# Attention by pairs of blocks in four 64x64 quadrants, the first two token tiles interleaved by quarters of the hidden units, and a new planned order

## The chip, the core and the metric

The kernel runs on one core of a Trainium2 chip. The engines are TensorE (PE in the profile, its weight loads PEld), VectorE (DVE), ScalarE (ACT), GpSimd (POOL) and SyncE (SP), which issues the DMAs. The metric is the device time of one launch in microseconds: 595.18 us, the median of three runs (594.43 to 595.61).

## The reference, cut to what matters

Two computations follow each other. A linear attention with per-channel decay runs over 4 batches, 8 heads, 768 tokens and 48 channels; its output, 3072 tokens by 384 channels, goes through a feed-forward layer of 2048 hidden units with a rational activation. All of it is float32.

```python
for t in range(S):
    cur = np.einsum('bhd,bhe->bhde', u[None] * kt, vt)
    y[:, :, t] = np.einsum('bhd,bhde->bhe', rt, state + cur)
    state = w[None, :, :, None] * state + np.einsum('bhd,bhe->bhde', kt, vt)
...
h = x @ w_in                      # 384 -> 2048
P = a[0] + a[1] * h + a[2] * h2 + a[3] * h3
Q = 1.0 + np.abs(b[0]) * np.abs(h) + np.abs(b[1]) * h2
return ((P / (Q + 1e-06)) @ w_out).astype(np.float32)
```

## The kernel before

**Attention.** A block is 128 tokens of one batch; there are 24, numbered so that blocks n and n+1 with n even are the same stretch of two batches, and block n+4 continues block n. For a block, k and r are scaled by powers of the decay (`scale_k`, `scale_r`), transposed on TensorE (`trans`: four 128x128 transposes into tk or tr) and copied out of PSUM (`trk_ev`, `trr_ev`). `a_pe` multiplies k by r within sub-blocks of 64 tokens: 16 small products per block, heads in pairs, one head of a pair in rows 0 to 63 of the array and the other in rows 64 to 127, each into the opposite half of the output partitions. `a_ev` masks the result (L452). `kv_pe` (L472, L473) forms k times v for the first 64 tokens and then again for all 128; `kv_ev` adds the old state (L487); `y_pe` (L500) multiplies by state and masked scores together; `y_ev` (L505) adds the bonus term, which `bonus_a`, `bonus_b`, `bonus_sum` and `bonus_v` make (L396, L401, L406, L410). `carry` (L511) decays the state for the next block of the batch. Small float32 matmuls show as two records each in the trace.

**Weights.** The weights come in as 64-bit floats. 28 pieces (12 of w_in, 16 of w_out) are loaded, turned into float32 by integer steps on ScalarE, VectorE and GpSimd, and split into a high and a low part (`cv_...`; L282 and L306 are two of the steps). `pieces` has them in four groups of seven, one group for each quarter of the hidden units.

**Feed-forward layer.** Two blocks make a token tile of 256 tokens, 12 tiles. A tile is worked through in 8 units `SL[s]` of 256 hidden units (JG = 2 groups of 128), 96 units in all, of which the last is split in two. Per unit: `f1` (18 matmuls of 128x256 per half of it, nine each, L541), five steps on ScalarE (z, q, t, ln, ex), five on VectorE (u3 L596, hi L602, p L606, d L612, lo L616) and `f2` (12 matmuls of 128x384, L545 to L547), which adds into two PSUM banks o0 and o1 over the 8 units of a tile; then `put_out` (L650, L652) copies them out and `put_dma` stores them. x is transposed and split for each tile by `xt_pe`, `xt_hi`, `xt_lo`.

**Order.** All of this is a list of tasks with a priority number, an estimated cost, dependencies and buffers. `run()` plays it through as a list scheduler: whenever an engine is free, the task of smallest number that fits is taken. The result is a fixed order on each engine, which the engine then follows in order; at run time each instruction waits on semaphores. Tasks that two engines could do go to the one that takes them first. While nothing else is ready, small bf16 matmuls into o1 ("warm", L1009) are put on TensorE until the first f2. The tables `AT` (blocks), `CT` (pieces), `OFF` (kinds of task) and `X0`, `DX0` to `DX2` (units) hold the numbers. `GFREE` and `GTIME` decide whether the step lo goes to GpSimd; with `GTIME` at 754.72 all 97 go to VectorE.

```python
p_ = pat("a", n)
o = slice(p * P + e * HALF, p * P + (e + 1) * HALF)
nc.tensor.matmul(p_[HALF:P, o], kt[0:HALF, p, c], ya[0:HALF, p, c], start=True, stop=True)
nc.tensor.matmul(p_[0:HALF, o], kt[HALF:P, p, c], yb[HALF:P, p, c], start=True, stop=True)
```

Of the kernel before, what the change touches and what calls it, by code (L numbers as in the profile page):

```python
# [30 lines left out]


@with_exitstack
def tile_linear_attention_rational_ffn(ctx, tc, r, k, v, w, u, w_in, w_out, a, b, out):
# [286 lines left out]
    rh, kh, ysa, ysb, vs = ([], [], [], [], [])  # L321
    vs2 = [cst.tile([P, 5, 2, NP, D], F32, name=f"vs{i}") for i in range(B // 2)]
    for i in range(3):
        for lst, nm in ((rh, "rh"), (kh, "kh")):
            lst.append(cst.tile([P, NP, 2, HALF], F32, name=f"{nm}{i}"))
    kt = cst.tile([P, NP, P], F32, name="kt")
    for i in range(2):
        for lst, nm in ((ysa, "ysa"), (ysb, "ysb")):
            lst.append(cst.tile([P, NP, P], F32, name=f"{nm}{i}"))
# [24 lines left out]
    def att_load(n, what):  # L354
# [5 lines left out]
        else:  # L360
            t, src = (hv(kh[n % 3]), k) if what == "k" else (hv(rh[n % 3]), r)
# [32 lines left out]
    def bonus_a(n, e):
        m = at.tile([P, H, D], F32, tag="m", name=f"m{n}", bufs=NM)
        e.tensor_mul(m, hv(rh[n % 3]), hv(kh[n % 3]))  # L396
# [15 lines left out]
    def trans(n, src, nm):  # L412
        p_ = pat(nm, n)
        for p in range(NP):
            nc.tensor.transpose(p_[:, ts(p, P)], src[:, p].rearrange("t a d -> t (a d)"), ident)  # L415
# [5 lines left out]
    def trk_ev(n, e):  # L421
        copy(e, kt.rearrange("p a t -> p (a t)"), state[n]["tk"])

    def trr_pe(n):
        trans(n, rh[n % 3], "tr")

    def trr_ev(n, e, half):
        y_, rows = ((ysa, slice(0, HALF)), (ysb, slice(HALF, P)))[half]
        copy(e, y_[n % 2][rows].rearrange("p a t -> p (a t)"), state[n]["tr"][rows])

    def a_pe(n):
        p_ = pat("a", n)
        ya, yb = ysa[n % 2], ysb[n % 2]
        for p in range(NP):
            for e in range(2):
                c = slice(e * HALF, (e + 1) * HALF)
                o = slice(p * P + e * HALF, p * P + (e + 1) * HALF)
                nc.tensor.matmul(p_[HALF:P, o], kt[0:HALF, p, c], ya[0:HALF, p, c], start=True, stop=True)  # L438
                nc.tensor.matmul(p_[0:HALF, o], kt[HALF:P, p, c], yb[HALF:P, p, c], start=True, stop=True)
        state[n]["a"] = p_  # L440

    def a_rows(n, half):
        return ((ysa[n % 2], slice(HALF, P)), (ysb[n % 2], slice(0, HALF)))[half]


    def a_ev(n, half, e):
        y_, rows = a_rows(n, half)
        av = state[n]["a"][rows]
        if e is nc.scalar:
            copy(e, y_[rows].rearrange("p a t -> p (a t)"), av)  # L450
            return
        nc.vector.tensor_mul(  # L452
            y_[rows].rearrange("p a (e t) -> p (a e) t", e=2), av.rearrange("p (c t) -> p c t", t=HALF),
            mask[rows].unsqueeze(1).to_broadcast([HALF, 2 * NP, HALF]),
        )

    def a_mask(n, half):
        y_, rows = a_rows(n, half)
        yv = y_[rows].rearrange("p a t -> p (a t)")
        nc.gpsimd.affine_select(  # L460
            yv, yv, pattern=[[0, 2 * NP], [1, HALF]], base=-1, channel_multiplier=-1,
            compare_op=ALU.is_ge, fill=0.0,
        )

    def kv_pe(n):
        d = state[n]
        p_ = pat("kv", n)
        k_, v_ = kh[n % 3], d["v"]
# [665 lines left out]
```

## Time and profile before

| | |
|---|---|
| median of the runs | 595.18 us |
| span of the profiled execution, first to last instruction | 593.4 us |
| TensorE busy, share of the span | 563.1 us, 95% |
| VectorE busy | 517.7 us, 87% |
| ScalarE busy | 435.5 us, 73% |
| GpSimd busy | 166.5 us, 28% |

The profiled execution's span is 1.8 us below the median of the runs. "Busy" is the time in which at least one instruction of the engine ran; matmuls are pipelined, so that a matmul's own duration is longer than the distance to the next one's start, and it is that distance that a row of matmuls costs. The mean durations of a group are of single instructions.

### The profile page before, as it was taken

Reading aid. Unit: us, or ns where it says so; the run is one execution under the profiler, and the core shown is the slowest. Engines: PE = TensorE matmul, PEld = TensorE weight load, DVE = VectorE, ACT = ScalarE, POOL = GpSimd, SP = SyncE. Lnnn points to the kernel's source line nnn. Section 1 sums busy time; section 2 is a strip of 40 time slices with the busy share of each in tenths; the row PEclk is TensorE's granted clock in tenths of the full one; section 3 lists DMA queues with packets and bytes.
Section 4 is the critical chain, followed back from the end, with each engine's and each line's share of the span. In section 5 each row is a group of like instructions: output and inputs, shape, how many; then the busy total and the mean of one; then the engine's idle time right before and its main releaser. Section 6 shows DMA issues by size and latency. Waiting matters only on the chain.

```text
span 593.4 us, 14638 instructions
## 1 busy us (share of the span) xinstructions
PE 563.1 (95%) x5991; PEld 540.8 (91%) x5991; DVE 517.7 (87%) x825; ACT 435.5 (73%) x729; POOL 166.5 (28%) x189
## 2 busy tenths in 40 slices
PE   8899696789999999999999999999999999999995
PEld 8799585778999999999999999999999999999995
DVE  5999998999999997889899888898888998888882
ACT  7679876978862785777677878865778785888780
POOL 6698976664135121013040010143001010000000
PEclk9999888989999999999999999999999999999999
DMA  7687653551222230012020003021003000000000
GB/s 189 163 224 193 166 142 92 127 109 32 55 53 57 68 75 8 2 41 54 28 55 2 27 1 73 10 42 43 14 0 81 2 15 15 0 28 2 28 1 31
DMA packets 95807, 34.85 MB, mean 59 GB/s; under 512 B 89074, under 2 KB 92148, under 8 KB 95732
## 3 DMA queue, kind: packets, MB, share of 16 engines
q1 hardware_dynamic: 95732, 33.83, 23.4%
q8 instruction: 49, 0.80, 0.6%
q14 instruction: 26, 0.21, 0.1%
HBM read 29.11 MB, written 4.72 MB: 57 GB/s over the span
## 4 chain that ended last, share of the span: by engine, by line
PE 71%; DVE 3%; ACT 1%; issue 1%
PE h L541 29%; PE o L545 11%; PE o L546 10%; PE o L547 10%; PE y L500 2%; PE a L438 2%; PE kv L472 2%; PE x L519 1%; PE tk L415 1%; PE tr L415 1%; DVE h L596 1%; DVE q L606 0%; DVE g L602 0%; DVE vs L511 0%; ACT t L583 0%
## 5 line engine op out<-in xcount | busy, mean ns | idle before, releaser
L541 PE MATMUL h<-xth,wi_hi 128*128 128x256 f32 x576 | 166.2, 289 | 0.0
L541 PE MATMUL h<-xtl,wi_hi 128*128 128x256 f32 x576 | 161.6, 281 | 0.0
L541 PE MATMUL h<-xth,wi_lo 128*128 128x256 f32 x576 | 161.5, 280 | 0.0
L545 PE MATMUL o<-wo_hi,g 128*128 128x384 f32 x384 | 134.8, 351 | 0.0
L547 PE MATMUL o<-wo_hi,g 128*128 128x384 f32 x384 | 130.4, 339 | 1.4 <-DVE g L616 1.4
L546 PE MATMUL o<-wo_lo,g 128*128 128x384 f32 x384 | 130.1, 339 | 0.0
L572 ACT ACTIVATE q<-h 128x512 f32<-128x512 f32 (+1 forms) x97 | 57.4, 591 | 83.3 <-PE h L541 63.0
L541 PEld LDWEIGHTS h<-xth,wi_hi 128*128 128x128 f32 x576 | 109.0, 189 | 1.2
L541 PEld LDWEIGHTS h<-xtl,wi_hi 128*128 128x128 f32 x576 | 109.2, 190 | 0.0
L541 PEld LDWEIGHTS h<-xth,wi_lo 128*128 128x128 f32 x576 | 108.8, 189 | 0.0
L602 DVE SCALAR_TENSOR_TENSOR g<-h,sig,z 128x512 fp32r<-128x512 f32 (+1 forms) x97 | 72.0, 743 | 28.1 <-ACT z L592 25.8
L578 ACT ACTIVATE w<-q,off,root 128x512 f32<-128x512 f32 (+1 forms) x97 | 75.8, 781 | 2.9 <-DVE q L606 2.7
L596 DVE SCALAR_TENSOR_TENSOR h<-t,sig,h 128x512 f32<-128x512 f32 (+1 forms) x97 | 72.0, 742 | 3.2 <-ACT t L583 2.9
L583 ACT ACTIVATE t<-h,off,root 128x512 f32<-128x512 f32 (+1 forms) x97 | 74.7, 770 | 0.1
L547 PEld LDWEIGHTS o<-wo_hi,g 128*128 128x128 f32 x384 | 72.6, 189 | 2.4 <-DVE g L616 2.4
L612 DVE SCALAR_TENSOR_TENSOR h<-h,sig,q 128x512 f32<-128x512 f32 (+1 forms) x97 | 72.7, 750 | 2.3
L606 DVE SCALAR_TENSOR_TENSOR q<-w,sig,g 128x512 f32<-128x512 f32 (+1 forms) x97 | 72.1, 743 | 2.6
L545 PEld LDWEIGHTS o<-wo_hi,g 128*128 128x128 f32 x384 | 72.6, 189 | 1.4
L546 PEld LDWEIGHTS o<-wo_lo,g 128*128 128x128 f32 x384 | 72.7, 189 | 0.0
L592 ACT ACTIVATE z<-z,lnb 128x512 f32<-128x512 f32 (+1 forms) x97 | 69.9, 721 | 2.3
L588 ACT ACTIVATE z<-w,lnb 128x512 f32<-128x512 f32 (+1 forms) x97 | 66.4, 685 | 3.6 <-POOL wi_lo L306 1.1
L616 DVE TENSOR_TENSOR g<-h,z 128x512 fp32r<-128x512 f32 (+1 forms) x97 | 65.7, 679 | 0.7
(147 smaller groups left out, 932.0 us busy)
## 6 DMA issues: line engine op xcount, KB each, us to landing
sto<-in_moe_w_out_dram SPq DMA_DIRECT2D x16, 384.0 KB, 3.7
sti<-in_moe_w_in_dram SPq DMA_DIRECT2D x12, 512.0 KB, 5.2
rh<-in_r_dram SPq DMA_DIRECT2D x24, 192.0 KB, 3.7
kh<-in_k_dram SPq DMA_DIRECT2D x24, 192.0 KB, 3.3
vn<-in_v_dram SPq DMA_DIRECT2D x24, 192.0 KB, 3.4
out_dram<-os SPq DMA_DIRECT2D x24, 192.0 KB, 1.9
vs<-in_v_dram SPq DMA_DIRECT2D x24, 96.0 KB, 3.5
wraw<-in_w_dram SPq DMA_DIRECT2D x1, 1.5 KB, 2.3
```

The costliest lines, as they stand in the source:

```text
L541: nc.tensor.matmul(o, wt_[:, cc, ts(j, P)], x_[:, cc], start=(n == 0), stop=(n == 3 * NCC - 1))
L545: nc.tensor.matmul(o, hi, wo_hi[:, j], start=(j == 0), stop=False)
L546: nc.tensor.matmul(o, hi, wo_lo[:, j], start=False, stop=False)
L547: nc.tensor.matmul(o, lo, wo_hi[:, j], start=False, stop=(j == NJ - 1))
L578: nc.scalar.activation(g["w"], w_, AF.Square, scale=RB, bias=KB)
L583: nc.scalar.activation(g["t"], g["h"], AF.Square, scale=RA, bias=KA)
L588: nc.scalar.activation(g["z"], g["w"], AF.Ln, scale=2.0 ** -LN_SHIFT, bias=lnb[:, 2:3])
L592: nc.scalar.activation(g["z"], g["z"], AF.Exp, scale=-1.0, bias=lnb[:, 1:2])
L596: nc.vector.scalar_tensor_tensor(g["h"], g["t"], KAP, g["h"], op0=ALU.add, op1=ALU.mult)
L602: nc.vector.scalar_tensor_tensor(g["hi"], g["h"], c0, g["z"], op0=ALU.add, op1=ALU.mult)
L606: nc.vector.scalar_tensor_tensor(g["q"], g.get("w", g["q"]), qe, g["hi"].bitcast(F32), op0=ALU.add, op1=ALU.mult)
L612: nc.vector.scalar_tensor_tensor(g["d"], g["h"], c0, g["q"], op0=ALU.add, op1=ALU.subtract)
```

## The change

**Pairs and quadrants.** Attention tasks are per pair of blocks (m = 0 to 11) where they were per block. `a_pe(m)` issues 32 products: for both blocks, four head pairs, two sub-blocks e and two heads q, with head q's rows 0 to 47 or 64 to 111 of the array and the output in the half of the partitions that e gives, in one PSUM bank per head. So four successive products lie in four different 64x64 quadrants; before, two successive ones lay in two. `kv_pe(m)` issues 32 products of the same kind (two sub-blocks by two heads); the sum over 128 tokens is not formed by the array any more but by a second `kv_ev` step. The last pair of each batch pair (m = 10, 11) needs only the first sub-block, 16 products. `a_ev` is four steps per pair of 64x512, `kv_ev` four of 48x384, `carry` two of 48x384; before it was two per block in each case, `carry` with 48x192. Transposes give 112 rows, not 128. `y_pe`, the bonus steps, scaling and loads stay per block. r has two buffers, not three.

**Interleaving.** Units 0 to 15, two tiles' worth, go quarter by quarter: two units of tile 0, two of tile 1, two of tile 0 and so on. f2 opens and closes its accumulation at each change of tile: `put_out` then copies a partial output to SBUF (tag m) or adds to it there, 16 steps for these two tiles where it was 4. f1 waits only for the pieces of w_in, f2 for those of w_out.

**Order.** `order_of` replaces `run()`: the same kind of list scheduler with numbers of its own in `PRM`, a bonus `MB` for staying in a tile mode, and `SIDE`, which names the units (20 to 96) whose step lo goes to GpSimd. For these `ew_d` writes to SBUF.

```diff
+ 'DG': 7.55,
...
+ 'NT': 2,
...
+ 'X': (158.93, 16.6, 7.22, 6.95)}
...
+            bonus = prm["MB"] if e == "P" and mode else 0.0
+            ranked = sorted((key[i] - (bonus if tasks[names[i]]["mode"] == mode else 0.0), i) for i in ready[e])
+            i = next((i for _, i in ranked if allowed(i, e, now)), None)
...
-    def a_pe(n):
...
+    def a_pe(m):
+        ps = [pat("a", (m, q)) for q in range(2)]
+        for x in range(2):
+            for p in range(NP):
+                for e in range(2):
+                    c = ts(e, HALF)
+                    for q in range(2):
+                        nc.tensor.matmul(
+                            ps[q][c, ts(x * NP + p, HALF)], kt[RROWS[q], x, p, c], ys[q][RROWS[q], x, p, c], start=True, stop=True
+                        )
...
+    def kv_pe(m):
+        last = m // 2 == NB - 1
+        ps = [pat("kv", (m, e)) for e in range(1 if last else 2)]
...
+                for e, p_ in enumerate(ps):
+                    for q in range(2):
+                        nc.tensor.matmul(
+                            p_[RROWS[q], ts(x * NP + p, D)], k_[ts(e, HALF), 2 * p + q], v_[ts(e, HALF), 2 * p + q], start=True, stop=True
+                        )
...
+        pv, dst = state["kv", m, e][RROWS[q]], s_[:, chain[e + 1]]
+        if m < 2 and e == 0:
+            copy(on, dst, pv)
         else:
...
+            nc.vector.tensor_add(dst, pv, s_[:, chain[e]])
...
-    SL = [(f, j, JG) for f in range(NTILE) for j in range(0, NJ, JG)]
+    NSEG = 4
+    SEG = NJ // NSEG
+    SL = [(f, j, JG) for g in range(NSEG) for f in range(NT) for j in range(g * SEG, (g + 1) * SEG, JG)] if NT > 1 else []
+    SL += [(f, j, JG) for f in range(NT if NT > 1 else 0, NTILE) for j in range(0, NJ, JG)]
...
+    def put_out(s, hf, e):
+        f, j0, nj = SL[s]
+        o_ = ops[f][hf][:, 0:DM]
+        if (f, hf) in oss:
+            nc.vector.scalar_tensor_tensor(oss[f, hf], o_, SG, oss[f, hf], op0=ALU.mult, op1=ALU.add)
+            return
...
-            add(("lo", s), lambda e, s=s: ew_lo(s, e), t + 8, {"D": 0.1 + 0.53 * x, "G": 0.15 + 1.08 * x}, [("d", s)], use=[h, ("q", s), ("z", s), ("g", s)])
+            side[s] = s in PRM["SIDE"]
+            add(("lo", s), lambda e, s=s: ew_lo(s, e), t + 8, {"G": 0.15 + 1.08 * x} if side[s] else {"D": 0.1 + 0.53 * x}, [("d", s)],
```

Three places show what moves. The first is TensorE. In the program before, after the second f2 half of a unit (o_1) stand the 16 scores products of one block, L438 and L439 in turn, of which the last two are shown, then f2, f1 and the products of kv.

```order
L438 MATMUL a_1612<-ysa_115,kt 64x64
L439 MATMUL a_1612<-ysb_116,kt 64x64
L545 MATMUL o_1_1599<-wo_hi,g_1494 128x384
...
L541 MATMUL h_1646<-xth_937,wi_hi 128x256
...
L472 MATMUL kv_1691<-vn_1409,kh_113 48x48
L473 MATMUL kv_1691<-vn_1409,kh_113 48x48
```

In the changed program, at the third pair of blocks, kv(2, 0) and kv(2, 1) are the two sub-blocks' banks and a(2, 0) and a(2, 1) the two heads'; 16 rows of kv (each x2) and 32 of a stand together.

```order
L774 MATMUL o_1_1882<-wo_hi,g_1859 128x384
L705 MATMUL kv(2, 0)_1982<-vn_1821,kh_111 48x48 x2
L705 MATMUL kv(2, 1)_1983<-vn_1821,kh_111 48x48 x2
...
L675 MATMUL a(2, 0)_2024<-ys_114,kt 64x64
L675 MATMUL a(2, 1)_2025<-ys_115,kt 64x64
...
L772 MATMUL o_0_2064<-wo_hi,g_1935 128x384
```

Two blocks' products now stand in one group, in which each four go to four quadrants. The second place is VectorE around the third unit (its u3 is the first row of L596 or L834). Before, h, g and q are of units, kt and ysa of later blocks' attention, kv of the state, bitsi and bitso of weights:

```order
L596 SCALAR_TENSOR_TENSOR h_1646<-t_1826,sig,h_1646 128x512
L487 TENSOR_TENSOR vs_107<-kv_1809,vs_107 48x2x192
L602 SCALAR_TENSOR_TENSOR g_1837<-h_1646,sig,z_1757 128x512
L487 TENSOR_TENSOR vs_107<-kv_1809,vs_107 48x2x192
L606 SCALAR_TENSOR_TENSOR q_1708<-w_1714,sig,g_1837 128x512
L282 TENSOR_SCALAR bitsi_2_1862<-cp_1832 128x512
L612 SCALAR_TENSOR_TENSOR h_1646<-h_1646,sig,q_1708 128x512
L452 TENSOR_TENSOR ysa_117<-a_1844,mask 64x512
L309 COPY kt<-tk_1868 128x512
L452 TENSOR_TENSOR ysb_118<-a_1844,mask 64x512
L616 TENSOR_TENSOR g_1837<-h_1646,z_1757 128x512
```

In the changed program the same unit:

```order
L834 SCALAR_TENSOR_TENSOR h_1275<-t_1356,sig,h_1275 128x512
L515 TENSOR_SCALAR bitsi_0_1395<-cp_1378 128x512
L898 TENSOR_SCALAR os_0_1406<-o_0_1331,sig 128x384
L542 CAST wi_hi<-bitsi_2_1370 128x512
L840 SCALAR_TENSOR_TENSOR g_1411<-h_1275,sig,z_1390 128x512
L844 SCALAR_TENSOR_TENSOR q_1353<-w_1372,sig,g_1411 128x512
L850 SCALAR_TENSOR_TENSOR h_1275<-h_1275,sig,q_1353 128x512
L515 TENSOR_SCALAR cp_1418<-cp_1418 128x512
L854 TENSOR_TENSOR g_1411<-h_1275,z_1390 128x512
```

No attention stands between its steps, only weights and a partial output. The third place is GpSimd in the second third of the program. Before, its queue holds attention steps alone (kh and rh the scaling, m the bonus, vs the state):

```order
L388 TENSOR_TENSOR kh_113<-kh_113,wkn 128x8x48
L392 TENSOR_TENSOR rh_112<-rh_112,wrn 128x8x48
L396 TENSOR_TENSOR m_2801<-rh_112,kh_113 128x384
L401 TENSOR_TENSOR m_2801<-m_2801,ub 128x384
L511 TENSOR_TENSOR vs_107<-vs_107,w_93 48x192 x2
```

In the changed program from unit 20 on the step lo (L854, g<-q,z) stands among them:

```order
L738 TENSOR_TENSOR vs_107<-vs_107,w_93 48x384 x2
L626 TENSOR_TENSOR kh_112<-kh_112,wkn 128x8x48
L854 TENSOR_TENSOR g_2826<-q_2764,z_2799 128x512
L630 TENSOR_TENSOR rh_108<-rh_108,wrn 128x8x48
L634 TENSOR_TENSOR m_2915<-rh_108,kh_112 128x384
L626 TENSOR_TENSOR kh_109<-kh_109,wkn 128x8x48
L639 TENSOR_TENSOR m_2915<-m_2915,ub 128x384
L630 TENSOR_TENSOR rh_110<-rh_110,wrn 128x8x48
L854 TENSOR_TENSOR g_2883<-q_2801,z_2848 128x512
```

An lo now stands behind a scaling that waits for a load, and f2 of its unit waits for the lo.

Counted in the two orders ahead of the 21st unit's first VectorE step: score masks 28 before and 12 after, additions to the state 20 and 12, bonus sums 15 and 8, additions of the bonus 13 and 6, bonus products 11 and 4, decays of the state 7 and 1, scalings 9 and 2, copies 32 and 22, low parts of weights 12 and 6, splits of x 8 and 6, output copies 2 and 14, steps d and lo of earlier units 19 and 20 each. Behind the 21st unit's first matmul stand, before and after: groups of score products 10 (of a block) and 9 (of a pair), groups of kv 10 and 9 (two of them half), y 11 and 18, groups of four transposes 19 and 34, groups of three transposes of x 16 and 18, units of f2 80 and 78.5.

More of the change, by code (lines that the diff above doesn't have):

```diff
@@ L324, in tile_linear_attention_rational_ffn @@
         for lst, nm in ((rh, "rh"), (kh, "kh")):
[L325 to L329, printed above, removed]
+            if i < 2 or nm == "kh":
+                lst.append(cst.tile([P, NP, 2, HALF], F32, name=f"{nm}{i}"))
+    kt = cst.tile([P, 2, NP, P], F32, name="kt")
+    ys = [cst.tile([P, 2, NP, P], F32, name=f"ys{q}") for q in range(2)]
+    RROWS = (slice(0, D), slice(HALF, HALF + D))
+    AROWS = (slice(HALF, P), slice(0, HALF))
     for i in range(B):
@@ L360, in att_load @@
         else:
[L361 removed]
+            t, src = (hv(kh[n % 3]), k) if what == "k" else (hv(rh[n % 2]), r)
         nc.sync.dma_start(t, src[bi, :, c, :].rearrange("h t d -> t h d"))
@@ L421, in trk_ev @@
     def trk_ev(n, e):
-        copy(e, kt.rearrange("p a t -> p (a t)"), state[n]["tk"])
+        copy(e, kt[0:TR, n % 2].rearrange("p a t -> p (a t)"), state[n]["tk"][0:TR])
     def trr_pe(n):
[L425 to L429, printed above, removed]
-    def a_pe(n):
[L432 to L440, printed above, removed]
@@ L457, in a_mask @@
[L457 to L468, printed above, removed]
-        pv = p_[:, 0 : 2 * NP * D].rearrange("p (e a d) -> p e a d", e=2, a=NP)
-        for e, rows in ((0, slice(0, HALF)), (1, slice(0, P))):
-            for p in range(NP):
-                nc.tensor.matmul(pv[0:D, e, p], k_[rows, p, 0, 0:D], v_[rows, 2 * p], start=True, stop=True)
-                nc.tensor.matmul(
-                    pv[HALF : HALF + D, 1 - e, p], k_[rows, p, 1, 0:D], v_[rows, 2 * p + 1], start=True, stop=True
-                )
-        d["kv"] = pv
@@ L777, in build @@
+        lastf = {SL[s][0]: s for s in range(NS)}
         for s in range(NS):
@@ new lines, in build @@
+                new = [("o", ("o", s))] if first and hf == 0 else []
+                so = max(s_ for s_ in range(s + 1) if SL[s_][0] == f and opens(s_))
+                wo_ = [("co", p0 + 3 + (j0 + jj) % 4) for jj in range(nj)]
+                prev = ("f2", s, 0) if hf else ("f2", s - 1, 1) if s else None
+                add(("f2", s, hf), lambda e, s=s, hf=hf: f2(s, hf), t + 5.5 + hf * 0.1, {"P": 1.06 * x}, [("lo", s), prev, *wo_],
+                    new=new, use=[("g", s)] + ([] if new else [("o", so)]), cols=2304 * x)
@@ new lines, in build @@
+                if closes(s):
+                    done = j0 + nj == NJ
+                    some = so > min(s_ for s_ in range(NS) if SL[s_][0] == f)
+                    buf = ("os", f, hf)
+                    prv = [("os", max(s_ for s_ in range(s) if SL[s_][0] == f and closes(s_)), hf)] if some else []
+                    add(("os", s, hf), lambda e, s=s, hf=hf: put_out(s, hf, e), t + 6, {"D": 0.53} if some else {"A": 0.37, "D": 0.53}, [("f2", s, hf), *prv],
+                        new=[] if some else [("os" if done else "m", buf)], use=[("o", so)] + ([buf] if some else []))
+                    if done:
+                        add(("od", f, hf), lambda e, f=f, hf=hf: put_dma(f, hf), t + 7, {"S": 0.6}, [("os", s, hf)], use=[buf])
@@ L1007, in run @@
+    prologue()
+    build()
+    order, tag_of, _ = order_of(tasks, tags, CAP, PRM)
+    bank.update(tag_of)
+    warm = ps_o.tile([P, 512], F32, tag="o1", name="warm")
+    with tc.manual_schedule():
         for n_, e in order:
-            if n_[0] == "warm":
+            if n_ == "warm":
                 nc.tensor.matmul(warm[:, 0:P], wones, wones, start=True, stop=True)
             else:
-                tasks[n_]["fn"](ENG.get(e))
-    with tc.manual_schedule():
-        run()
+                fns[n_](ENG.get(e))
```

649 lines of the change are left out of this document (359 added, 290 removed), and 6 rows, old and new, of the table OFF.

## The prediction

> **What bounds the kernel now.** I read the busy time by stages first. The stages are cut at the first matmul of f1 (57.4 us), at the first f1 matmul of the 21st unit (206.3 us), at 400 and at 580 us. Columns: stretch, its length, then busy time and instructions of TensorE, its weight loads, VectorE, ScalarE and GpSimd, the granted TensorE clock, the DMA share, GB/s.
>
> ```profile
> core 0: us, PE busy (x) PEld busy (x) DVE busy (x) ACT busy (x) POOL busy (x), PEclk, DMA share, GB/s
> 0.00:57.40 57.40, 52.78 (x973) 49.18 (x973) 48.44 (x89) 43.77 (x90) 43.39 (x56) 1.00 0.77 198
> 57.40:206.30 148.90, 130.18 (x1578) 119.77 (x1576) 139.00 (x225) 108.50 (x191) 80.45 (x84) 0.94 0.38 90
> 206.30:400.00 193.70, 193.70 (x1887) 188.19 (x1886) 171.40 (x264) 145.50 (x231) 32.83 (x38) 1.00 0.14 32
> 400.00:580.00 180.00, 179.80 (x1531) 177.36 (x1528) 155.78 (x244) 137.16 (x217) 9.81 (x11) 1.00 0.07 19
> ```
>
> Up to 206.3 us VectorE is busy 187.4 us and TensorE has holes, filled only in part by warm matmuls; behind it TensorE is busy 373.5 of 373.7 us and VectorE 327.2. So there are two stages: one that VectorE's work sets, with 19 us of its own waits, and one that TensorE's work sets. That the cut is at the 21st unit shows in the same view kept to f1's line and to the line of u3, the unit's first VectorE step.
>
> ```profile
> core 0 of [0], span 593.4 us
> 0.00:206.30 206.30, 50.05 (x361) 46.05 (x362) 0.96 0.49 120
> 0.00:212.05 212.05, 14.94 (x20) 0.96 0.48 118
> ```
>
> 20 units of 18 matmuls are 360, and the 361st starts the 21st unit; 20 of its u3 steps stand ahead of 212.05 us. The forecast moves this point and then re-weighs the TensorE work behind it. That remainder now is 593.4 - 206.3 = 387.1 us.
>
> **Change, first stage: VectorE's work ahead of the 21st unit.** Durations per instruction are in these groups (mean in ns before the second bar).
>
> ```profile
> L452 DVE TENSOR_TENSOR ysa<-a,mask 64x512 f32<-64x512 f32 x24 | 16.7, 695 | 2.4 <-PE a L439 1.6
> L487 DVE TENSOR_TENSOR vs<-kv,vs 48x384 f32<-48x384 f32 x40 | 22.1, 552 | 4.8 <-PE kv L473 4.4
> L406 DVE TENSOR_REDUCE dt<-m 128x8 f32<-128x384 f32 x24 | 13.1, 544 | 0.2
> L505 DVE TENSOR_TENSOR m<-y,m 128x384 f32<-128x384 f32 x24 | 13.2, 549 | 0.3
> L396 DVE TENSOR_TENSOR m<-rh,kh 128x384 f32<-128x384 f32 x7 | 4.8, 685 | 0.1
> L511 DVE TENSOR_TENSOR vs<-vs,w 48x192 f32<-48x192 f32 x9 | 7.0, 783 | 0.1
> L388 DVE TENSOR_TENSOR kh<-kh,wkn 128x384 f32<-128x384 f32 x5 | 3.7, 737 | 0.0
> L309 DVE COPY ysa<-tr 64x512 f32<-64x512 f32 x9 | 6.1, 676 | 0.1
> L306 DVE TENSOR_TENSOR wo_lo<-bitso,wo_hi 128x384 fp32r<-128x384 f32 x7 | 5.9, 838 | 2.3 <-ACT wo_hi L309 2.3
> L652 DVE TENSOR_SCALAR os<-o,sig 128x384 f32<-128x384 f32 x9 | 5.5, 613 | 4.7 <-PE o L547 4.7
> ```
>
> By the counts of the two orders the change takes out of this stretch 16 masks at 0.69 (11.0 us), 8 additions to the state at 0.552 (4.4), 7 bonus sums at 0.544 (3.8), 7 additions of the bonus at 0.549 (3.8), 7 bonus products at 0.685 (4.8), 6 decays at 0.783 (4.7), 7 scalings at 0.737 (5.2), 10 copies at about 0.68 (6.8), 6 low parts at 0.838 (5.0) and 2 splits of x at the 0.55 of the bonus row (1.1): 50.6 us. It puts in 12 output copies at 0.613 (7.4) and one d and one lo more (1.4): 8.8 us. Net 42 us. Most of it isn't gone but deferred: attention of blocks 6 to 14, which the old order did early. The means of the decay, the scaling and the low parts hold waiting: 48x192 elements at 0.783 us stand beside 48x384 at 0.552. With these 19 and the 7 bonus products priced at 0.55 the net is 36 us. I take the middle, 39.
>
> Not all of it comes through. ScalarE, which has only 108.5 us of work in 148.9 us before, loses less of its work; by the two orders its instructions and VectorE's ahead of the ninth unit then add up to about equal sums, so one cannot hide behind the other. I add 4 us to the 19 us that VectorE waits now; the bounds are 12 us less (only waits like those of the start left) and 8 us more. The 21st unit's u3 comes at 212.05 - 39 + 4 = 177 us and its f1 at 206.3 - 35 = 171.3 us. The weights' loads are no bound there: the DMA engines are busy 0.77 in the first 57.4 us and 0.38 behind, and the changed order asks for fewer blocks early.
>
> **Change, second stage: TensorE's work behind the 21st unit's f1.** What one group costs is its distance from start to start. The two pieces of the timeline are one block's kv group and one block's a group, each 32 records, with the next matmul that isn't theirs.
>
> ```profile
> 224.45 0.24 PE L472 MATMUL kv<-vn,kh 64*48 64x48 f32 x1
> 224.46 0.24 PE L473 MATMUL kv<-vn,kh 64*48 64x48 f32 x1
> 224.53 0.20 PE L472 MATMUL kv<-vn,kh 64*48 64x48 f32 x1
> ...
> 225.44 0.45 PE L545 MATMUL o<-wo_hi,g 128*128 128x384 f32 x1
> ...
> 227.28 0.34 PE L546 MATMUL o<-wo_lo,g 128*128 128x384 f32 x1
> 227.45 0.34 PE L547 MATMUL o<-wo_hi,g 128*128 128x384 f32 x1
> 227.72 0.27 PE L438 MATMUL a<-ysa,kt 64*64 64x64 f32 x1
> 227.73 0.27 PE L439 MATMUL a<-ysb,kt 64*64 64x64 f32 x1
> ...
> 228.80 0.45 PE L545 MATMUL o<-wo_hi,g 128*128 128x384 f32 x1
> ```
>
> kv costs 225.44 - 224.45 = 0.99 us and a 228.80 - 227.72 = 1.08 us. Within them two records start within 0.01 us, one in each of two tiles, and the next follows 0.07 us later; 32 records in 0.99 us are 16 steps of two at 0.06. The pair's group has 64 records, so 16 steps of four if four quadrants run as two tiles do now. Then a pair costs what a block does now. If they do not, it costs twice that. Four starts at the 0.01 us shown take 0.04 us, less than a step, so I take the first; the second is a rival. The last two pairs' kv have half the records and use two tiles: 0.99 all the same.
>
> One rule speaks against it. The Trainium skill ("TensorE: Matmul & The Clock Gate", Part 1, "Wait — 56ns, not 53.3ns?") says that starts never come closer than about 25 ns. Here 32 records in 0.99 us already average 31 ns with their entry, and single starts are 10 ns apart, so in the trace the rule does not hold across tiles. By it a step of four would take 100 ns, each full group some 0.7 to 0.9 us more, and the estimated time would be about 12 us above mine.
>
> The other prices: one y group, and one group of four transposes, up to the start of the f1 behind it, whose second matmul comes 0.21 us later where 0.12 is the rule.
>
> ```profile
> 214.37 1.07 PE y L500 x32
> 207.31 0.60 PE L415 MATMUL tk<-identw,kh 128*128 128x128 f32 x4
> 207.66 0.36 PE L541 MATMUL h<-xth,wi_hi 128*128 128x256 f32 x1
> 207.87 0.28 PE L541 MATMUL h<-xtl,wi_hi 128*128 128x256 f32 x1
> 207.99 0.28 PE L541 MATMUL h<-xth,wi_lo 128*128 128x256 f32 x1
> ```
>
> y is 1.07 us, four transposes 0.35 + 0.09 = 0.44 us; three transposes of x I estimate at three quarters, 0.33. A unit of f2 is 12 matmuls; eleven steps lie between 225.44 and 227.45, so all are 2.2 us. How much of each stands behind the cut now, the same view by stages shows for the lines of a, y, transposes and f2:
>
> ```profile
> 206.30:593.50 387.20, 11.41 (x160) 10.04 (x160) 1.00 0.11 26
> 206.30:593.50 387.20, 12.46 (x352) 11.16 (x352) 1.00 0.11 26
> 206.30:593.50 387.20, 11.55 (x76) 8.98 (x76) 1.00 0.11 26
> 206.30:593.50 387.20, 110.81 (x320) 60.06 (x320) 1.00 0.11 26
> ```
>
> That is 10 groups of a (16 records of L438 each), 11 of y, 19 of four transposes, 80 units of f2 (4 of L545 each); with 10 of kv and 16 of x from the order: 10.8 + 9.9 + 11.8 + 8.4 + 5.3 = 46.2 us. After, by the order: 9 a (9.7), 9 kv (8.9), 18 y (19.3), 34 transposes (15.0), 18 x (5.9) = 58.8 us, less 1.5 units of f2 (3.3) = 55.5. The remainder grows by 9 us to 396 us: the deferred attention lands here, and the quadrants pay for about two thirds of it. Without them it would grow by 9 x 1.08 + 7 x 0.99 = 17 us more.
>
> VectorE must keep up there. It had 327.2 of 373.7 us. It now gets the deferred steps (36 to 42 us less the 9 of added ones and weights), and loses 77 steps lo, one of five in each unit, to GpSimd. That is a net loss, so TensorE stays the bound; around tile 3 to 5, where three pairs' steps come together, I allow 2 us (0 to 6). GpSimd's price for lo is nearest to its other product-like step of this size, and its queue has room: 32.83 + 9.81 us of work in 374, plus 77 times 1.4.
>
> ```profile
> L306 POOL TENSOR_TENSOR wi_lo<-bitsi,wi_hi 128x512 fp32r<-128x512 f32 x7 | 9.8, 1395 | 4.8 <-ACT wi_hi L309 4.8
> L388 POOL TENSOR_TENSOR kh<-kh,wkn 128x384 f32<-128x384 f32 x19 | 20.0, 1052 | 70.3 <-DMA kh<-in_k_dram 68.8 <-PE tk L415 1.1
> ```
>
> The longer lo (1.395 against a VectorE step of some 0.7) is covered by the f1 of the next unit; uncovered at the very end it costs below 1 us. Sixteen closings of f2 hold the next opening of the same bank for one copy of 0.613 us; f1 of the other tile covers them, else 10 us in the first stage, which VectorE's bound hides.
>
> **Sum.** 171.3 + 396 + 2 = 569.3 us of span, plus the 1.8 us by which the median lies above the profiled span: 571 us.
>
> **Rivals.** (1) *Quadrants that share rows or columns do not overlap.* For: no row shows four tiles. Against: a's two tiles share neither rows nor columns, kv's share rows, and both run in step. A group then costs twice: 571 + 17 = 588 us. The Trainium skill (same page, Part 3, "What overlaps and what doesn't") says that a weight load overlaps matmuls in flight only where row groups differ, which gives this case. In the trace L473's matmul starts 0.01 us behind L472's on the same rows, which the rule doesn't fit. Chance 0.08.
>
> (2) *GpSimd's queue, in order, holds the lo.* The scaling of k, before which GpSimd waits 70.3 us over 19 times, 3.7 us each, now stands ahead of an lo; f2 waits, and TensorE runs out of f1 after about one unit's (2.1 us by nine matmuls' 0.12 twice over). Two scalings per pair are 7.4 us of waiting; if 5.3 us of it per pair are uncovered, nine pairs lose 48 us, and the time is 619 us; if half of that, 595. It decides from 24 / 9 = 2.7 us per pair. Against: the loads stand early in SyncE's queue, and a wait for data that isn't wanted yet is idle time without a price. Chance of a result above 594: 0.09.
>
> (3) *VectorE's waits shrink.* Attention out of the early stretch also takes out what VectorE waited for there. With 12 us fewer waits and all 42 us: 571 - 4 - 12 = 555 us. Chance 0.13.
>
> (4) *The deferred work lands where VectorE becomes the bound*: 6 us and more in the middle, 575 to 583 us; part of the range.
>
> **How the numbers follow.** The forecast, with its own bounds of 558 to 584, has 0.70; rivals (1) to (3) have 0.08, 0.09 and 0.13. The range of 556 to 592 takes in (1) and the near part of (3). A measurement of this kernel can tell about 0.2% (1.2 us) from no change. Only rival (2), or (1) together with lost waits, reaches that band: faster 0.88, same 0.03, slower 0.09.
>
> **What would show it.** In the changed profile: the first matmul of the 21st unit near 171 us, TensorE without holes behind it, kv and a groups of 64 records in about 1 us with four starts per step, GpSimd's lo near 1.4 us with the f2 of its unit not waiting for it. Wrong would be: groups of 2 us (rival 1), f2 released by GpSimd for more than some 20 us in total (rival 2), or a VectorE that is still full at the 30th unit.

## The result and the profile after

The changed kernel takes 568.5 us (median of 4 runs, 567.77 to 570.07), the kernel before 594.8 us in the same comparison: a ratio of 0.956, interval 0.954 to 0.958. The profiled execution has a span of 567.0 us, 1.5 us below the median. The forecast was 571.

The busy time by stages of the changed kernel, cut at its first f1 matmul (50.18 us) and at the first f1 matmul of its 21st unit (165.34 us). Columns as in the prediction: TensorE, its weight loads, VectorE, ScalarE, GpSimd, the granted clock, the DMA share, GB/s.

```profile
50.18:165.34 115.16, 100.42 (x903) 94.76 (x902) 101.69 (x164) 101.14 (x174) 60.94 (x57) 0.97 0.34 92
165.34:400.00 234.66, 229.64 (x2768) 221.38 (x2767) 199.44 (x305) 165.62 (x270) 123.07 (x115) 1.00 0.26 53
400.00:555.00 155.00, 154.57 (x1364) 152.94 (x1363) 119.44 (x188) 117.82 (x184) 61.16 (x53) 1.00 0.08 21
```

The same view kept to f1's line, and to the line of u3:

```profile
0.00:165.35 165.35, 47.65 (x361) 45.47 (x361) 0.98 0.44 117
0.00:173.47 173.47, 14.94 (x21) 0.98 0.46 117
```

The 361st f1 matmul, the 21st unit's first, starts at 165.3 us, where it was at 206.3: 41 us earlier. From there to the end are 566.97 - 165.34 = 401.6 us, where there were 387.2: 14.5 us more. In that stage TensorE, which had lost 0.2 us before, is idle 5.0 us up to 400 and 0.4 behind. Between 50 and 165 us three engines are busy for about the same time: TensorE 100.4, VectorE 101.7, ScalarE 101.1 of 115.2 us.

Each kernel's row up to its 21st unit, first of the kernel before, then of the changed one:

```profile
0.00:206.25 206.25, 182.90 (x2546) 168.90 (x2547) 187.39 (x313) 152.27 (x280) 123.84 (x140) 0.96 0.49 120
```

```profile
0.00:165.34 165.34, 140.83 (x1726) 131.34 (x1727) 145.38 (x244) 135.01 (x243) 98.16 (x107) 0.98 0.44 117
```

VectorE's work up to that point fell from 187.4 to 145.4 us, and what it waits there went from 18.9 to 20.0. The prediction counted VectorE's work up to a later point, the 21st unit's u3. The rows up to there, before and after:

```profile
0.00:212.07 212.07, 188.72 (x2619) 174.48 (x2619) 191.96 (x319) 157.90 (x290) 124.86 (x141) 0.96 0.48 118
```

```profile
0.00:173.46 173.46, 148.95 (x1845) 139.15 (x1846) 153.19 (x258) 141.77 (x256) 101.83 (x111) 0.98 0.46 117
```

A group of scores of one pair, piece of TensorE's timeline in the changed kernel (start, duration; a(6, 0) and a(6, 1) are the banks of the two heads):

```profile
245.97 0.22 PE L675 MATMUL a(6, 0)_3722<-ys,kt 48*64 48x64 f32 x1
246.01 0.22 PE L675 MATMUL a(6, 1)_3723<-ys,kt 48*64 48x64 f32 x1
246.02 0.22 PE L675 MATMUL a(6, 0)_3722<-ys,kt 48*64 48x64 f32 x1
246.02 0.22 PE L675 MATMUL a(6, 1)_3723<-ys,kt 48*64 48x64 f32 x1
246.03 0.22 PE L675 MATMUL a(6, 0)_3722<-ys,kt 48*64 48x64 f32 x1
246.07 0.22 PE L675 MATMUL a(6, 1)_3723<-ys,kt 48*64 48x64 f32 x1
...
246.78 0.22 PE L675 MATMUL a(6, 1)_3723<-ys,kt 48*64 48x64 f32 x1
```

Four start within 0.02 us, and the next four 0.06 us after the first of them. The trace's own stamps have starts 7 ns apart and a step of 59 ns, for kv 45 ns. Those are the steps of the blocks before, in which two started. 64 records take from 245.84 to 246.78, 0.94 us.

GpSimd: the row of its lo from the costliest groups, and from the list of waits (total, times, longest) what it waited for and what the last f2 product of a unit waited for.

```profile
L854 POOL TENSOR_TENSOR g<-q,z 128x512 fp32r<-128x512 f32 (+1 forms) x77 | 99.0, 1285 | 178.3 <-DVE q L850 145.6
```

```profile
POOL g L854 <- DVE q L850: 145.6, 50, 6.4
POOL kh L626 <- DMA kh<-in_k_dram: 20.1, 2, 17.1
PE o L774 <- DVE g L854: 6.2, 7, 2.5
```

An lo on GpSimd takes 1.285 us. What GpSimd waits for is mostly VectorE's step d, so its queue is ahead of the work. The two waits for a load of k lie ahead of the 21st unit. f2 waits only for lo steps of VectorE, all ahead of the 21st unit.

### The profile page after: what moved, and what is told of

It is laid out like the page before. It is cut to its first block, busy times and chain, and to the rows that moved or that the text cites. A ratio compares the mean times of both kernels' runs of the same rounds, so it can differ in the third digit from the quotient of the medians.

```text
span 567.0 us, 14579 instructions
## 1 busy us (share of the span) xinstructions
PE 532.2 (94%) x5891; PEld 512.5 (90%) x5891; DVE 467.5 (82%) x742; ACT 420.6 (74%) x700; POOL 283.9 (50%) x276
## 4 chain that ended last, share of the span: by engine, by line
PE 56%; DVE 20%; ACT 12%; POOL 5%; issue 3%; DMA 1%; SPq 1%; DVEq 0%; POOLq 0%; ACTq 0%
PE h L768 25%; PE o L772 8%; PE o L774 8%; PE o L773 8%; DVE ys L689 4%; PE y L729 3%; DVE vs L718 3%; DVE g L840 2%; DVE q L844 2%; DVE ys L542 1%; ACT z L830 1%; DVE q L850 1%; ACT z L826 1%; ACT cp L509 1%; ACT t L821 1%
## 5 line engine op out<-in xcount | busy, mean ns | idle before, releaser
L854 POOL TENSOR_TENSOR g<-q,z 128x512 fp32r<-128x512 f32 (+1 forms) x77 | 99.0, 1285 | 178.3 <-DVE q L850 145.6
L768 PE MATMUL h<-xth,wi_hi 128*128 128x256 f32 x576 | 164.1, 285 | 3.8 <-DVE q L844 3.8
L834 DVE SCALAR_TENSOR_TENSOR h<-t,sig,h 128x512 f32<-128x512 f32 (+1 forms) x97 | 72.1, 743 | 4.7 <-ACT t L821 4.2
L850 DVE SCALAR_TENSOR_TENSOR q<-h,sig,q 128x512 f32<-128x512 f32 (+1 forms) x77 | 57.1, 742 | 2.1
## 6 DMA issues: line engine op xcount, KB each, us to landing
kh<-in_k_dram SPq DMA_DIRECT2D x24, 192.0 KB, 3.4
rh<-in_r_dram SPq DMA_DIRECT2D x24, 192.0 KB, 3.4
vn<-in_v_dram SPq DMA_DIRECT2D x24, 192.0 KB, 3.5
out_dram<-os SPq DMA_DIRECT2D x24, 192.0 KB, 1.9
```

The source lines that it names most:

```text
L768: nc.tensor.matmul(o, wt_[:, cc, ts(j, P)], x_[:, cc], start=(n == 0), stop=(n == 3 * NCC - 1))
L834: nc.vector.scalar_tensor_tensor(g["h"], g["t"], KAP, g["h"], op0=ALU.add, op1=ALU.mult)
L854: e.tensor_mul(g["lo"], g["d"], g["z"])
```

## The experiments

"Behind the cut" means from the 21st unit's first f1 matmul to the end. TensorE's cost of a kind of work there is the sum of the distances from each matmul to the next, with gaps left out; the holes are those gaps. Ratios are to the kernel before.

| kernel | median us | ratio, interval | 21st unit's f1, us | VectorE idle up to there, us | holes behind, us |
|---|---|---|---|---|---|
| before | 594.8 | 1 | 206.3 | 18.9 | 0.2 |
| changed | 568.5 | 0.956 (0.954 to 0.958) | 165.3 | 20.0 | 5.5 |
| two_quadrants | 570.57 | 0.958 (0.956 to 0.961) | 165.7 | | 2.3 |
| one_quadrant | 585.06 | 0.983 (0.981 to 0.985) | 167.7 | | 1.2 |
| two_quadrants_long | 573.69 | 0.963 (0.960 to 0.966) | 166.2 | | 1.6 |
| lo_on_vector | 578.43 | 0.973 (0.969 to 0.976) | 164.0 | 19.0 | 13.9 |
| vector_plus | 571.52 | 0.961 (0.959 to 0.964) | 166.4 | 16.5 | 6.3 |
| scalar_plus | 574.25 | 0.966 (0.964 to 0.968) | 167.6 | 23.3 | 5.9 |
| no_interleaving | 599.79 | 1.009 (1.007 to 1.011) | 195.2 | 38.7 | 12.3 |
| before_late | 624.54 | 1.049 (1.046 to 1.051) | 188.3 | 49.9 | 10.5 |
| before_late_inter | 617.3 | 1.038 (1.035 to 1.041) | 186.7 | 45.5 | 8.6 |
| inter_lo | 622.34 | 1.046 (1.044 to 1.048) | 189.5 | | 9.6 |
| inter_tile2_early | 612.61 | 1.029 (1.026 to 1.032) | 182.0 | 32.2 | 8.4 |
| before_vector_plus | 599.46 | 1.007 (1.005 to 1.010) | 211.7 | 17.4 | 0.2 |

**Quadrants.** The first run leaves the order of tasks as it is and changes the order of products within a group.

```diff
             for p in range(NP):
-                for e in range(2):
+            for d, p in ((d, p) for d in range(2) for p in range(NP)):
                     for q in range(2):
+                        e = q ^ d
```

> The changed kernel with its order of tasks kept; only the order of the products inside a group of scores and a group of kv differs, so that every two successive products lie in two quadrants and not every four in four. Theory (quadrants overlap in fours, and TensorE is the bound behind the 21st unit): a group of 64 score records takes about 2.15 us in place of 1.11 and one of kv 1.9 in place of 0.95; 9 groups of scores, 7 full ones of kv behind the cut give 9 x 1.05 + 7 x 0.95 = 16 us more, 584.5 us; the 21st unit's f1 stays within 3 us of 165.3, since the three early pairs' extra 6 us fall into TensorE's holes. Rival (TensorE has slack between 165 and 345 us, where the chain runs over VectorE and GpSimd): half of it, about 576 us. Second rival (the array runs such products one by one whatever their place): no change, 568.5 us.

Measured: 570.57 us, only 2 us more. A group of scores costs 13.6 / 9 = 1.51 us where it costs 10.0 / 9 = 1.11; all kv behind the cut 9.8 us where it was 7.6. So the theory's 16 us of work came out as 5.8, of which the holes took 3.2 and shorter y groups 1.7. The edit was too weak: the pair of quadrants changed after every eight products, and the starts in the trace show fours within 22 ns among the twos.

The second run puts the loops over q and e outside, so that four successive products (eight records; the expectation's "eight successive products" is wrong in this) lie in one quadrant.

> As the run with two quadrants, but eight successive products lie in one and the same quadrant. If the distance between two products of one quadrant is the 0.06 us that a step of two took before, a group of 64 records takes 3.9 us: 9 x 2.8 + 8 x 3.0 = 49 us more behind the cut, 617 us. If the array overlaps a row of products into one quadrant as well, the time stays at 568.5 us.

Measured: 585.06 us, 16.6 more. Scores cost 23.3 us behind the cut and kv 16.1, in all 21.8 more than in the changed kernel. So place matters: the array does not run such products at the same pace whatever their place. The 49 us were an overestimate, since quadrants that follow each other overlap here too. Four records from the middle of a group of kv, of two banks and so of two quadrants, show two starting together:

```profile
249.02 0.21 PE L705 MATMUL kv(6, 0)_3660<-vn,kh 64*48 64x48 f32 x1
249.06 0.20 PE L705 MATMUL kv(6, 1)_3661<-vn,kh 64*48 64x48 f32 x1
249.06 0.20 PE L705 MATMUL kv(6, 0)_3660<-vn,kh 64*48 64x48 f32 x1
249.10 0.20 PE L705 MATMUL kv(6, 1)_3661<-vn,kh 64*48 64x48 f32 x1
```

A longer row in the same two quadrants is the proper undoing (loop d outermost, over both blocks; kv with e outermost).

> The changed kernel, order of tasks kept, products in two quadrants at a time, and now 16 products in a row in the same two (in the run two_quadrants the pair changed after every eight, and the trace shows records of the next pair starting among them). If a quadrant takes one score record per 59 ns and one kv record per 45 ns, as the steps of the traces say, a group of scores has 32 steps and takes 2.0 us in place of 1.1, a full group of kv 1.6 in place of 0.85: 9 x 0.95 + 7 x 0.75 = 14 us more TensorE work behind the cut, of which up to 5 fill its holes: 577 to 583 us. If the quadrants are not what makes the groups short: 570 us as in the run two_quadrants.

Measured: 573.69 us. A piece of its timeline, the first products of a group of scores:

```profile
248.01 0.24 PE L676 MATMUL a(6, 0)_3722<-ys,kt 48*64 48x64 f32 x1
248.02 0.27 PE L676 MATMUL a(6, 1)_3723<-ys,kt 48*64 48x64 f32 x1
248.09 0.22 PE L676 MATMUL a(6, 0)_3722<-ys,kt 48*64 48x64 f32 x1
248.12 0.22 PE L676 MATMUL a(6, 1)_3723<-ys,kt 48*64 48x64 f32 x1
248.15 0.22 PE L676 MATMUL a(6, 0)_3722<-ys,kt 48*64 48x64 f32 x1
248.18 0.22 PE L676 MATMUL a(6, 1)_3723<-ys,kt 48*64 48x64 f32 x1
```

Two starts in each 0.06 us, where the changed kernel has four. Scores cost 16.6 us (1.85 a group) and kv 11.6, together 10.6 us more work than the changed kernel, where 14 were expected; the time is 5.2 us longer, less than the 577 to 583 us expected and more than the 570 of the other theory. The rest went into the holes (5.5 to 1.6) and into y (20.4 to 18.3). Work on TensorE behind the cut is thus not passed on one to one: the stage has some 5 us of slack that such work fills first, 5.4 us here and 5.2 in one_quadrant (21.8 us of work, 16.6 of time).

**lo back on VectorE,** order of tasks kept:

```diff
-        e.tensor_mul(g["lo"], g["d"], g["z"])
+        nc.vector.tensor_mul(g["lo"], g["d"], g["z"])
```

> The changed kernel, its order of tasks kept, with the step lo of units 20 to 96 on VectorE at the same places. VectorE then has 53 us more behind the cut: 375 of 402. If VectorE's room is needed there, as the prediction has it (the chain of waits runs over VectorE and GpSimd from 165 to 345 us): TensorE gets 5 to 15 us of holes, 574 to 583 us. If TensorE's work alone sets that stage (the run inter_lo gained nothing from lo on GpSimd): within 2 us of 568.5.

Measured: 578.43 us, 9.9 more. Busy time behind the cut, and TensorE's longest waits there:

```profile
164.00:576.00 412.00, 393.22 (x4168) 382.14 (x4166) 369.11 (x576) 285.40 (x457) 91.93 (x92) 1.00 0.18 39
```

```profile
PE y L729 <- DVE ys L689: 4.5, 9, 1.2
PE kv(7, 0)_4125 L705 <- DVE kt L542: 1.5, 1, 1.5
```

VectorE is busy 369.1 of 412.0 us, and TensorE gets 13.9 us of holes, nearly all before work of attention; 8.7 us of them end on VectorE's steps (masked scores, copies) and 3.7 on ScalarE's. The first theory holds: VectorE's room is needed there, though over the stage it is busy only 90%.

**What sets the first stage.** A step that changes nothing is added to each of the first 20 units, on VectorE behind u3:

```diff
+        if s in range(20):
+            nc.vector.tensor_reduce(spare, ub, axis=mybir.AxisListType.X, op=ALU.add)
```

> The changed kernel with its order kept, and behind u3 of each of units 0 to 19 one more step on VectorE, a sum over 128x384 of constants (0.55 us), 11 us in all. If VectorE's sum sets the first stage: the 21st unit's f1 10 to 11 us later, 579 us. If the arrival of the weights and the chain of each unit set it, with 20 us of VectorE idle beside: 3 to 5 us later, 572 us.

Measured: 20 steps of 0.546 us, 10.9 us in all; the 21st unit's f1 came 1.1 us later, the time is 571.52 us, 3.0 more. On ScalarE, ahead of t, a copy of 0.508 us:

> The same on ScalarE: ahead of t of each of units 0 to 19 one more copy of 128x384 constants (about 0.48 us), 9.6 us in all. If VectorE alone sets the first stage: at most 2 us later, 570 us. If ScalarE is as close (101 us busy of 115 between the first f1 and the 21st unit's, as VectorE): 5 to 10 us later, 574 to 579 us.

Measured: 10.2 us in all; 2.3 us later, 574.25 us, 5.8 more. The profiled execution is the fastest of its four, and its span is only 3.1 us longer than the changed kernel's; the rest is not explained. Their rows up to the 21st unit:

```profile
0.00:166.40 166.40, 143.24 (x1726) 132.32 (x1727) 149.91 (x263) 135.49 (x243) 98.46 (x107) 0.99 0.44 116
```

```profile
0.00:167.60 167.60, 142.56 (x1726) 132.48 (x1727) 144.27 (x244) 143.66 (x262) 98.98 (x107) 0.98 0.44 115
```

Neither engine alone sets this stage in the changed kernel. The rows show how much the steps really added: VectorE's busy time up to the unit grew by 4.5 us (145.4 to 149.9), not by 10.9, since neighbouring records overlap and some others are shorter in this execution; ScalarE's grew by 8.7 (135.0 to 143.7). About a quarter of each, 1.1 and 2.3 us, came through to the 21st unit. These are single profiles, and lo_on_vector, which changes nothing ahead of that unit, has it 1.3 us earlier. In the medians more came through, 3.0 and 5.8 us, and by its time scalar_plus lies in the range of the theory that ScalarE is as close as VectorE, so how far ScalarE is a bound stays open. The same VectorE steps in the kernel before:

> The kernel before with its order kept and the same 20 added VectorE steps (11 us) behind u3 of units 0 to 19 as in the run vector_plus. If VectorE's sum set the first stage before, as the prediction had it: 21st unit's f1 9 to 11 us later, 604 to 606 us. If not (in the changed kernel the same steps made it 1.1 us later): 1 to 3 us later, 596 to 598 us.

```profile
0.00:211.70 211.70, 186.47 (x2546) 171.91 (x2547) 194.27 (x332) 152.75 (x280) 124.50 (x140) 0.94 0.47 117
```

Measured: the 21st unit 5.5 us later, 599.46 us, between both expectations. Half of the steps' 10.9 us came through, but four fifths of the 6.9 us by which VectorE's busy time grew (187.4 to 194.3). So VectorE was most of a bound before, and much less of one after.

**Deferral alone.** The kernel before with later numbers for its blocks and nothing else:

```diff
-        -58.04, -15.07, -92, 10.74, 3.74, 13.3, 54.36, 77.06, 63.23, 117.64, 139.68, 107.22,
+        -58.04, -15.07, -92.00, 10.74, 144.74, 148.64, 188.97, 192.87, 215.36, 219.26, 240.35, 244.25,
```

> The kernel before, by blocks, without interleaving and without any lo on GpSimd; only the 24 numbers of the blocks are later, so that ahead of the 21st unit's u3 stand 12 masks and 6 additions of the bonus, as in the changed kernel. Theory (VectorE's work ahead of the 21st unit sets its time): its f1 comes 45 us earlier, near 162 us; behind it stand 8 groups more each of scores (1.08) and kv (0.97), 7 of y (1.07), 17 of four transposes (0.37), 1 unit of f2 less: 28 us more, so 387 + 28 = 415 us, and VectorE with 375 of them adds 5 to 15 us of TensorE holes: 584 to 594 us. Rival (the interleaving and not the deferral makes the early gain, since all the weights are needed by the ninth unit without it): the 21st unit stays above 185 us and the time goes above 605 us.

```profile
0.00:188.30 188.30, 155.90 (x1840) 146.98 (x1841) 138.44 (x233) 133.12 (x238) 91.72 (x104) 0.93 0.36 98
```

Measured: 624.54 us, 5% slower than before. VectorE's work ahead of the 21st unit fell by 49 us as wanted, but the unit came only 18 us earlier: VectorE's waits grew from 18.9 to 49.9. Behind the cut the work grew by 38 us and the holes by 10. The theory fails here, and both of the rival's marks were hit (the 21st unit above 185, the time above 605); that interleaving is what makes the early gain, as the rival has it, this run alone can't show.

**Interleaving.** First the changed kernel without it (NT 1, planned anew with the units' numbers kept):

```diff
- 'NT': 2,
+ 'NT': 1,
...
-        n = NT * NG
+        n = 2 * NG
```

> The changed kernel without interleaving: units run tile by tile from the start (NT 1), the units' numbers kept, the order planned anew. Ahead of the 21st unit's u3 stand 20 masks in place of 12 and 3 output copies in place of 14; VectorE's priced work there is 9.6 us larger, TensorE's work behind the cut about 9 us smaller (2 groups of scores, 1 of kv, 2 of y, 6 of transposes, half a unit of f2). Theory (only VectorE's sum counts): 21st unit's f1 at 175 us, time 568 us, within 5 us. Rival (interleaving is what lets the weights come late): the first units wait for weights, TensorE has 10 us and more of extra holes up to the ninth unit, time 578 to 590 us.

```profile
0.00:195.20 195.20, 157.71 (x2059) 147.49 (x2060) 156.51 (x259) 141.59 (x254) 110.28 (x120) 0.94 0.43 109
```

Measured: 599.79 us, 0.9% slower than the kernel before and beyond both expected times. The extra holes that the rival named are there: from the first unit's f1 to the ninth's TensorE is idle 24.4 us, where it is 10.4 in the changed kernel. VectorE's work up to the 21st unit is 11 us larger than in the changed kernel, near the 9.6 expected, but its waits double to 38.7 us. The starts of f1 in the trace show where. Without interleaving the first units of the four quarters start at 51.3, 74.0, 88.9 and 113.6 us, and two units lie between. With it they start at 50.2, 71.7, 99.3 and 127.3 us, and four lie between. So when the last quarter of w_in is there (its last low part ends at 113.7 and 128.2 us), 6 units have been started in the one and 12 in the other. The units behind come more slowly without interleaving: (195.2 - 113.6) / 14 = 5.8 us each, against (165.3 - 127.3) / 8 = 4.8; in the kernel before, (206.3 - 123.3) / 14 = 5.9. So of the 29.9 us between the two, half is the lead (six units at 4.8, less the 13.7 us by which the quarter comes later) and half the slower pace, 14 units at 1.1, whose cause was not looked for.

Then interleaving put into before_late, with the outputs added up in SBUF as in the changed kernel:

```diff
-    SL = [(f, j, JG) for f in range(NTILE) for j in range(0, NJ, JG)]
+    SEG = NJ // 4
+    SL = [(f, j, JG) for g in range(4) for f in range(2) for j in range(g * SEG, (g + 1) * SEG, JG)]
+    SL += [(f, j, JG) for f in range(2, NTILE) for j in range(0, NJ, JG)]
```

> The kernel of the run before_late (by blocks, late attention numbers, no lo on GpSimd) with one thing added: units 0 to 15 go quarter by quarter over two tiles, with partial outputs in SBUF, as in the changed kernel. Theory now (VectorE's sum is not the bound by itself: two units wait for each quarter of the weights, and interleaving gives each quarter four): the 21st unit's f1 comes near 168 us where it was at 188.3; behind it the same work as there, 434 us: 604 us. Rival (what was lost in before_late lies in the late attention itself, and interleaving only adds 12 output copies, 7 us of VectorE): the 21st unit at 188 to 195 us, 625 to 632 us.

Measured: 617.3 us, 21st unit at 186.7, neither the theory's nor the rival's. The 13th unit came 9 us earlier (133.9, where it was 143.1), but the 17th waited: its f1 started at 173.1, 24.5 us behind the 16th's. It is the first of the third tile, whose attention had been put late. So the run couldn't show what it was made for. With lo of units 20 to 96 on GpSimd as well:

> As the run before_late_inter, and the step lo of units 20 to 96 on GpSimd: all of the change but the pairs and quadrants (and the planner's own numbers). Theory: behind the cut VectorE falls from some 376 to 323 us of work, and the holes of TensorE (10.5) and the slower f1 and f2 (5 us) of before_late go: 15 us less than before_late_inter, about 589 us; against the changed kernel 20 us are then left for pairs and quadrants (18 groups of scores at 1.08 and 18 of kv at 0.97 against 17.6 us: 19 us). Rival (VectorE has room, lo on GpSimd brings nothing): the same time as before_late_inter. Rival (pairs and quadrants bring nothing): 570 us.

Measured: 622.34 us, 5 more and not 15 less, nearest to the first rival. VectorE's work behind the cut fell from 373.2 to 341.5 us, the holes stayed (8.6 and 9.6). In this order lo on GpSimd brings nothing, in the changed one it brings 9.9 us. With the third tile's two blocks early again and the others 20 us less late:

> As the run before_late_inter (by blocks, interleaved, no lo on GpSimd), but the two blocks of the third tile early and the others 20 us earlier than there. In before_late and before_late_inter the 17th unit's f1 started 15 and 24 us behind the 16th's, since the third tile's attention came late. Theory (interleaving makes the early gain if no tile is late): the 21st unit's f1 at 165 to 175 us, the work behind it 420 us and 8 us of holes: 595 to 605 us. Rival (interleaving gains nothing; the changed kernel's own numbers do): the 21st unit at 183 us and later, 612 us and more.

```profile
0.00:182.00 182.00, 152.90 (x1767) 144.67 (x1767) 149.75 (x252) 136.08 (x244) 89.28 (x101) 0.92 0.38 103
```

Measured: 612.61 us. The 17th unit no longer waits (165.6, behind 160.3), but the 13th comes only at 148.6. It did not wait for its quarter of w_in, whose last low part ends at 115.9; the last piece of w_out, for which only f2 waits, is done at 142.5 us where it is at 126.1 in the changed kernel. What held the 13th unit is not shown. The 21st unit at 182.0 us is 1 us from the rival's mark and 7 from the theory's, and the time is the rival's. Its work behind the cut is a count of what pairs and quadrants save: 9 pairs' scores and kv cost 18.7 + 17.8 us by blocks and 10.0 + 7.6 in the changed kernel, 18.9 us.

## Why the prediction was right, and where its steps were not

**The number.** The sum was 171.3 + 396 + 2 = 569.3 us of span; measured are 165.3 + 401.6 = 567.0. Two errors, 6.0 us too late at the cut and 3.6 us too little behind it, partly cancel; that the sum came nearer than its terms is in part luck.

**First stage, the size.** Up to the 21st unit's u3, where the prediction's count ends, VectorE's work fell by 38.8 us (192.0 to 153.2): the middle of the two prices, 39, was right. The 4 us added for new waits were 0.2 (20.1 to 20.3), so u3 came at 173.5 us and not at 177. The rest of the 6.0 us lies between f1 and u3: the prediction kept their distance of 5.8 us, and it became 8.1.

**First stage, the reason.** The step "one that VectorE's work sets, with 19 us of its own waits" is the one that failed. Had it held, before_late would have won 45 us there, vector_plus lost 10, before_vector_plus 10; they won 18, lost 1.1, lost 5.5 (the last two with VectorE's busy time up by only 4.5 and 6.9). The clearest is before_late: VectorE's work fell by 49 us and its waits grew by 31. That the waits stayed at 20 us in the changed kernel is thus no property of VectorE; the prediction took it for one, and that the number came out is luck. What the runs suggest, without taking it apart, is that several parts have to fit: attention is taken out, and interleaving has units ready to fill its place, four for each quarter of the weights that arrives. Where one of these was missing the time came out longer than before: deferral by itself (before_late), the whole change without interleaving (no_interleaving), deferral and interleaving without the rest and the new plan (inter_tile2_early). The prediction counted the deferred steps and never asked what else would be ready then. It spoke of interleaving only as output copies and 16 closings of f2.

**Second stage, the work.** Here the steps held, to about 2 us. By distances from start to start, scores, kv, y, transposes and x cost 10.0 + 7.6 + 20.4 + 13.6 + 5.0 = 56.6 us, forecast 58.8; before they cost 43.2 (the forecast's prices gave 46.2). f2 gives back 2.7 (3.3 were forecast), f1 takes 0.4: 11.1 us more, where 9 were forecast. What follows the last matmul to the end of the span is 2.0 us shorter (4.8, before 6.8), which is no term of the forecast and hides this miss. The busy sums by line, scores, kv, y and x:

```profile
165.34:567.00 401.66, 10.83 (x576) 9.53 (x576) 1.00 0.18 40
165.34:567.00 401.66, 8.44 (x512) 7.38 (x512) 1.00 0.18 40
165.34:567.00 401.66, 21.09 (x576) 18.93 (x576) 1.00 0.18 40
165.34:567.00 401.66, 8.94 (x54) 6.68 (x54) 1.00 0.18 40
```

576 score records are 9 groups of 64, and 512 of kv are 7 groups and two halves, as counted.

**Second stage, the holes.** 2 us were allowed, 5.5 came, within the 0 to 6, all but 0.4 us of them up to 400 us, where rival (4) had them. They are mainly twelve waits of up to 0.9 us ahead of work of attention, which end on steps of VectorE (2.2 us), ScalarE (1.1), GpSimd (0.9) and TensorE itself (0.9). lo_on_vector shows that they grow with VectorE's work: give it more, and they are 13.9.

**Quadrants, and rival (1).** A step of four takes the time of a step of two, as forecast, so a pair costs what a block did (scores 1.11 and 1.08). The 17 us put on this were 18.9 of TensorE's work. As time they are worth less: two_quadrants_long got 10.6 us of work back and lost 5.2, and one_quadrant got 21.8 us and lost 16.6, so that by estimate, with 5 us of slack filled first, 17 us of work would cost about 12 us of time; rival (1)'s 588 us was priced too high as well as not met. The rule of the Trainium skill ("TensorE: Matmul & The Clock Gate", Part 1, "Wait — 56ns, not 53.3ns?"), starts never closer than about 25 ns, does not hold in this trace: 7 ns between quadrants, 64 records in 0.94 us. The Trainium skill (same page, Part 3, "Measured speedup vs the span model") gives about 4 ns between tiles, which is nearer to it. The sentence of the Trainium skill (same page, Part 3, "What overlaps and what doesn't") that weight loads overlap only where row groups differ did not show as a price here: kv products of the same rows start 7 ns apart.

**GpSimd, and rival (2).** Not met: no f2 behind the cut waited for an lo on GpSimd, and both waits for loads of k lie early. lo took 1.285 us where 1.395 was taken.

**Rival (3)** needed 12 us fewer waits of VectorE; up to the 21st unit's f1 they grew by 1.1.

**What stays open.** No single engine was shown to set the first stage of the changed kernel. Slowing the weights' steps on GpSimd was not tried, and neither was interleaving with the old early attention, in which the four partial outputs would share the seven buffers of the bonus steps. In before_late_inter and inter_tile2_early the 13th unit started 24 and 33 us after its quarter of w_in was there (109.9 to 133.9 us, 115.9 to 148.6), so that the arrival of w_in may set the pace in the changed kernel (128.2 and 127.3 us) but not in these two. How much of the 41 us is due to the new plan's numbers and how much to interleaving isn't separated: no_interleaving used numbers made for the other order, and inter_tile2_early numbers made for neither.

## What to carry to other kernels

A stage whose busiest engine has 9% of idle time is not proven to be set by that engine: add a step to it that does nothing, and see how much busy time that adds and how much of it comes through, before a sum of its work is taken for a forecast. Work that is moved out of a stage shortens it only if other work is ready then; look for what that work waits for (in the changed kernel, quarters of weights). Small matmuls into distinct quarters of the array cost one step per four here (59 ns for scores), so group them so that neighbours lie in different quarters; a saving on TensorE is worth its size only beyond the slack that other waits leave, here some 5 us.

## What was not expected of the hardware

Between products in different quadrants the starts lie 7 ns apart, and a step takes 59 ns for scores (64 columns) and 45 ns for kv (48 columns), with two products in it or with four. With four products in a row in one quadrant a group of 64 records costs 2.58 us and not the 3.8 us of 64 steps of 59 ns; products of quadrants that follow each other overlap even when each has a row of its own, so that the weak undoing (two_quadrants) gave back only 0.40 us of a group where two_quadrants_long gave 0.74. The granted clock up to the 21st unit was 0.98 in the changed kernel, 0.96 before and 0.92 to 0.94 in before_late, no_interleaving, before_late_inter, inter_lo, inter_tile2_early and before_vector_plus; why was not looked into.
